# Convolution in column halves with products from SBUF, and a PSUM pool that hands out single banks or pairs

## The chip, the cores and the metric

The kernel runs on one core of one Trainium2 chip. The metric is the device time of one execution in microseconds (us). Each run executes a kernel several times, next to executions of the kernel before on the same chip. An execution is slow when it is over 1.5% above the fastest of its kernel. Ratios and intervals use the fast executions alone.

Words used below: TensorE (PE in the profile) multiplies matrices, PEld is its weight load; VectorE is DVE, ScalarE is ACT, GpSimd is POOL, SyncE is SP. PSUM is TensorE's output memory of eight banks; a bank holds 512 fp32 values per partition. An eviction is a copy of a result out of PSUM. FFN 1 is the feed-forward part's first matrix product, followed by GELU on ScalarE; FFN 2 is its second, followed by SiLU on ScalarE.

## The reference

It joins a long convolution (by FFT, over 2048 tokens and 640 columns) and a feed-forward part of 1728 hidden columns. Cut to what matters:

```python
xn = layernorm(x)                                   # x: 2048 x 640, bf16
k_shift = sum_t shift(k, t) * shift_k[t]            # 4 taps
kv  = k_shift * v
y   = irfft(rfft(kv, 4096) * rfft(ssm_k, 4096))[:2048] + kv * ssm_D
h   = gelu(xn @ w1 + b1)
g   = silu(h @ w2 + b2)
out = x + xn * y * g
```

A warning about correctness. With the given inputs, the reference's output equals x exactly in bf16: the added term is too small to change any element. So "correct" says nothing about the convolution.

## The kernel before

The FFT is done as matrix products in stages. Stage 1 transforms k and u (u is kv) from SBUF, and the results go through scratch memory in HBM (scrK, scrU) because the axes have to change places. Stage 2 transforms them further; VectorE multiplies the spectra; inverse stage 1 (i1) and, through a third scratch (scrC), inverse stage 2 (i2) follow. All operations stand in one list, and a string named ORDER fixes the engine and the order of each, and the slot of every buffer. The framework puts in the semaphores.

The parts that matter here:

```python
ps_t = [psum.tile([P, 2, 512], F32, name="ps%d" % i) for i in range(4)]   # 4 tiles of 2 banks
ps_pool = Pool(ps_t, name="ps")                      # every user takes a whole pair
...
def f1_pair(c, ft0):                                 # FFN 1: two groups, both banks of one pair
    ps = Buf(pool=ps_pool, parts=2)
    for i in range(2):
        ... matmuls of group ft0 + i into ps.v[0:M, i, :], then GELU from ps.v[0:M, i, :]
...
def f2(c, q):                                        # FFN 2: two groups into one pair, one SiLU over both
    ps = Buf(pool=ps_pool, parts=2)
    ...
    op("silu", "ACT", ... in_=ps.v[:, :, 0:H] ..., reads=[ps], writes=[sl])
...
    op("prod", "DVE", ... in0=ps.v[:, None, :, 0:w].to_broadcast([P, 2, 2, w]), in1=kin.v[...], op=ALU.mult)
    ...                                              # product with the u spectrum straight from PSUM
    def i1(...):                                     # inverse stage 1: four terms summed on TensorE
        for n_, (qi, m, tb) in enumerate(((0, 0, 0), (0, 1, 2), (1, 0, 2), (1, 1, 1))):
```

## Time and profile before

| | before |
|---|---|
| median, range in the rounds with the changed kernel | 215.74 us, 214.17 to 217.03 (4 executions) |
| span of the profiled execution, granted TensorE clock | 214.4 us, 0.967 |
| TensorE busy, idle | 179.4 us, 35.0 us |

The page gives the busy time of each engine with its share of the span, then the chain of work that ended last, then groups of instructions. A group reads: line, engine, operation, output<-input, shapes, count | busy us, mean ns of one | idle time before them and what ended it. From the page of the kernel before:

```profile
PE 179.4 (84%) x1660; PEld 90.4 (42%) x1660; DVE 166.2 (78%) x233; ACT 126.5 (59%) x163; POOL 37.6 (18%) x62
...
PE 58%; DVE 20%; DMA 11%; issue 5%; ACT 3%; POOL 0%; DVEq 0%; ACTq 0%; POOLq 0%
...
L617 DVE TENSOR_TENSOR k_all<-ps,k_all 128x1920 bf16<-128x1920 f32 (+1 forms) x22 | 45.5, 2093 | 20.1 <-PE ps L596 17.1
...
L420 ACT ACTIVATE hT<-ps,b_f 128x512 bf16<-128x512 f32 (+1 forms) x28 | 18.2, 685 | 11.0 <-PE ps L416 11.0
```

TensorE is busiest. L617 is the spectral product that the change takes apart; L420 is GELU in the paired form. The next view cuts the execution into three stretches (columns: start:end, length, busy us of each engine with the number of instructions, granted clock, DMA share, GB/s):

```profile
0.00:19.40 19.40, 7.41 (x52) 4.53 (x53) 16.04 (x43) 11.81 (x14) 8.99 (x19) 1.00 0.89 335
19.40:191.40 172.00, 160.24 (x1504) 78.72 (x1505) 130.66 (x157) 113.24 (x148) 28.57 (x44) 0.98 0.71 232
191.40:214.40 23.00, 11.76 (x107) 7.20 (x106) 19.54 (x34) 1.41 (x2) 0.00 (x0) 0.84 0.70 264
```

The first FFN matmul starts at 19.43 us. Start and tail are thin for TensorE. The middle is dense, 160.2 of 172.0 us.

### The profile page before, as it was taken

To read this page: it belongs to the slowest core of one execution; us is meant where nothing else is said; L and a number is where in the kernel's file an instruction comes from. 1 tells how busy PE (TensorE), PEld (TensorE's weight loads), DVE (VectorE), ACT (ScalarE), POOL (GpSimd) and SP (SyncE) were. 2 spreads that over 40 slices of the span, in tenths; PEclk is the share of its full clock that TensorE was granted. 3 is DMA by queue.
4 is the path that set the end of the run, shared out by engine and by line. 5 is a ranking of instruction groups with operands and counts; after the bars stand their busy time and mean duration, and the time that the engine had idled before them with its cause. 6 is when DMAs were issued, how large, how long until landed. Compare 5 with 4: busy or idle time off the path is not lost.

```text
span 214.4 us, 4137 instructions
## 1 busy us (share of the span) xinstructions
PE 179.4 (84%) x1660; PEld 90.4 (42%) x1660; DVE 166.2 (78%) x233; ACT 126.5 (59%) x163; POOL 37.6 (18%) x62
## 2 busy tenths in 40 slices
PE   0448999979988999998999899698999968999810
PEld 0314443633335665564443333233565523666500
DVE  6997998959889999964218997967756887029994
ACT  5298455877788977589554555868765764111100
POOL 7055000402252252324000020012100121100000
PEclk9999999999999999999999999999999995999985
DMA  5999998994379988949681749187980515599555
GB/s 165 373 418 412 413 356 203 361 387 172 144 214 369 242 247 206 255 151 343 214 276 27 250 144 303 27 272 257 292 278 6 199 49 192 160 415 409 207 199 198
DMA packets 28021, 52.54 MB, mean 245 GB/s; under 512 B 10081, under 2 KB 20834, under 8 KB 27874
## 3 DMA queue, kind: packets, MB, share of 16 engines
q1 hardware_dynamic: 23952, 35.89, 51.6%
q0 software_dynamic: 3904, 16.39, 20.3%
q8 instruction: 13, 0.21, 0.4%
q14 instruction: 6, 0.05, 0.1%
q10 hardware_dynamic: 146, 0.00, 0.0%
HBM read 31.95 MB, written 18.35 MB: 235 GB/s over the span
## 4 chain that ended last, share of the span: by engine, by line
PE 58%; DVE 20%; DMA 11%; issue 5%; ACT 3%; POOL 0%; DVEq 0%; ACTq 0%; POOLq 0%
PE ps L465 24%; PE ps L431 14%; PE ps L416 10%; DMA scrK<-mm 7%; DVE xn L656 5%; DVE k_all L617 5%; PE ps L629 4%; PE ps L596 3%; PE ps L497 3%; DMA x<-in_x_dram 2%; DVE stats L370 2%; DVE x L448 2%; DMA b_r<-in_b_dram 1%; DVE kT L448 1%; DVE mm L234 1%
## 5 line engine op out<-in xcount | busy, mean ns | idle before, releaser
L465 PE MATMUL ps<-w_sb,hT 128*128 128x320 bf16 x448 | 66.5, 303 | 1.4 <-ACT hT L420 0.8
L617 DVE TENSOR_TENSOR k_all<-ps,k_all 128x1920 bf16<-128x1920 f32 (+1 forms) x22 | 45.5, 2093 | 20.1 <-PE ps L596 17.1
L465 PEld LDWEIGHTS <-hT 128*128 128x128 bf16 x448 | 42.4, 99 | 24.5 <-issue 8.4
L234 ACT CAST mm<-ps 128x640 bf16<-128x640 f32 x55 | 35.1, 699 | 12.6 <-PE ps L497 6.9
L416 PE MATMUL ps<-xnT,w_sb 128*128 128x512 bf16 (+1 forms) x140 | 34.0, 393 | 1.9 <-ACT hT L420 1.6
L431 PE MATMUL ps<-xnT,w_sb 128*128 128x512 bf16 (+1 forms) x140 | 32.2, 380 | 0.6 <-ACT hT L439 0.5
L420 ACT ACTIVATE hT<-ps,b_f 128x512 bf16<-128x512 f32 (+1 forms) x28 | 18.2, 685 | 11.0 <-PE ps L416 11.0
L469 ACT ACTIVATE sl<-ps 128x640 bf16<-128x640 f32 x16 | 11.3, 707 | 21.5 <-PE ps L465 13.7
L439 ACT ACTIVATE hT<-ps,b_f 128x1024 bf16<-128x1024 f32 (+1 forms) x14 | 15.5, 1112 | 13.2 <-PE ps L431 13.1
L234 ACT CAST v_all<-ps 128x960 bf16<-128x960 f32 (+1 forms) x19 | 17.2, 947 | 9.0 <-PE ps L629 9.0
L416 PEld LDWEIGHTS <-w_sb 128*128 128x128 bf16 (+1 forms) x140 | 13.3, 101 | 20.0 <-issue 7.5
L638 POOL DMA_DIRECT2D scrC<-v_all x11 | 8.2, 749 | 73.0 <-ACT v_all L234 33.7
L431 PEld LDWEIGHTS <-w_sb 128*128 128x128 bf16 (+1 forms) x140 | 13.0, 98 | 18.0 <-issue 4.4
L234 ACT CAST k_all<-ps 128x960 bf16<-128x960 f32 (+1 forms) x16 | 14.2, 927 | 5.1 <-PE ps L596 4.1
L497 PE MATMUL ps<-kT,W 64*128 64x320 bf16 x64 | 8.9, 337 | 9.3 <-DMA kT<-in_kT_dram 8.3
L629 PE MATMUL ps<-k_all,tabs 32*64 32x480 bf16 (+1 forms) x352 | 13.3, 397 | 3.7 <-DVE k_all L617 1.9
L501 POOL DMA_DIRECT2D scrK<-mm x16 | 8.8, 550 | 42.8 <-ACT mm L234 35.3
L470 DVE TENSOR_TENSOR xn<-xn,sl 128x640 bf16<-128x640 bf16 x16 | 7.6, 484 | 9.9 <-ACT sl L469 9.9
L497 PEld LDWEIGHTS <-W 64*128 64x128 bf16 x128 | 4.8, 95 | 20.7 <-issue 11.6
L656 DVE TENSOR_TENSOR xn<-ps,xn 128x640 bf16<-128x640 f32 x16 | 12.6, 816 | 1.1 <-PE ps L652 1.1
L501 POOL DMA_DIRECT2D scrU<-mm x16 | 8.9, 556 | 19.0 <-ACT mm L234 14.7
L521 DVE TENSOR_TENSOR mm<-k_all,mm 128x2560 bf16<-128x2560 bf16 x8 | 11.9, 1490 | 0.2
(75 smaller groups left out, 176.7 us busy)
## 6 DMA issues: line engine op xcount, KB each, us to landing
scrK<-mm POOLq DMA_DIRECT2D x16, 320.0 KB, 6.6
scrU<-mm POOLq DMA_DIRECT2D x16, 320.0 KB, 3.3
k_all<-scrK SPq DMA_DIRECT2D x10, 480.0 KB, 3.9
v_all<-scrU SPq DMA_DIRECT2D x10, 480.0 KB, 4.7
scrC<-v_all POOLq DMA_DIRECT2D x10, 480.0 KB, 3.7
mm<-scrC SPq DMA_DIRECT2D x6, 640.0 KB, 6.4
kT<-in_kT_dram SPq DMA_DIRECT2D x4, 640.0 KB, 8.8
v_all<-in_v_dram SPq DMA_DIRECT2D x4, 640.0 KB, 7.1
```

The costliest lines, as they stand in the source:

```text
L234: (nc.scalar.copy if e == "ACT" else nc.vector.tensor_copy)(out=out_, in_=in_)
L416: nc.tensor.matmul(out=ps.v[0:M, i, :], lhsT=w1_sb[:, ft, t, 0:M], rhs=xnT_b[c].v[:, t, :], start=(t == 0), stop=(t == DT - 1))
L420: op("gelu", "ACT", lambda e, i=i, ft=ft, M=M: nc.scalar.activation(out=hT_b[c].v[0:M, ft, :], in_=ps.v[0:M, i, :], func=ACT.Gelu_apprx_ta ...
L431: nc.tensor.matmul(out=ps.v[0:M, i, :], lhsT=w1_sb[:, ft, t, 0:M], rhs=xnT_b[c + i].v[:, t, :], start=(t == 0), stop=(t == DT - 1))
L439: nc.scalar.activation(out=o, in_=s, func=ACT.Gelu_apprx_tanh, bias=b1_f[0:M, ft:ft + 1], scale=1.0)
L465: nc.tensor.matmul(out=ps.v[:, h, 0:H], lhsT=hT_b[c].v[0:M, ft, q * P:(q + 1) * P], rhs=w2_sb[0:M, ft, h * H:(h + 1) * H], start=(ft == 0) ...
L497: nc.tensor.matmul(out=ps.v[:, h, 0:H], lhsT=W[r, j, :], rhs=src[r, j, cs], start=True, stop=True)
L501: op("s1st" + kind, "POOL", lambda e: nc.gpsimd.dma_start(out=by_k1(scr)[:, 2 * j:2 * j + 2, :], in_=o.v), reads=[o], writes=[scr_b[j]], s ...
L521: op("kv2", "DVE", lambda e: tt(out=kt_t, in0=win(2, 2), in1=wbc(2, 2), op=ALU.mult), reads=kb + [wb_b], writes=[kvt_b])
L617: op("prod", "DVE", lambda e, ps=ps, qb=qb, kin=kin, w=w: nc.vector.tensor_tensor(out=qb.v[:, 0:4 * w].rearrange("p (i r w) -> p i r w", i ...
L629: nc.tensor.matmul(out=pc[g // 2].v[64 * r:64 * r + 64, g % 2, 0:w], lhsT=I1[tb][32 * g:32 * g + 32, :], rhs=qs[qi].v[32 * g:32 * g + 32, ...
L656: op("ym", "DVE", lambda e, j=j, ps=ps: nc.vector.tensor_tensor(out=hv(xn[:, j, :]), in0=ps.v[:, :, 0:H], in1=hv(xn[:, j, :]), op=ALU.mult ...
```

## The change

Its intent: let half of the columns go through the whole convolution while the other half is still being transformed; take the sum of the four inverse terms off TensorE by combining the products on VectorE; and use PSUM more finely, so that an FFN group of one bank no longer takes a pair. The schedule string is new throughout. The core of the diff, with cuts marked by "...":

```diff
+class Banks(Pool):
+    def __init__(self, pairs):
+        super().__init__([p[:, i, :] for p in pairs for i in range(2)])
+        self.pairs, self.flex = pairs, True
+
+    def view(self, slot, width):
+        return self.views[slot] if width == 1 else self.pairs[slot // 2]
...
     ps_t = [psum.tile([P, 2, 512], F32, name="ps%d" % i) for i in range(4)]
-    ps_pool = Pool(ps_t, name="ps")
+    banks = Banks(ps_t)
+    def pair():
+        return Buf(pool=banks, width=2)
+    def bank():
+        return Buf(pool=banks)
...
-    def f1_pair(c, ft0):
-        ps = Buf(pool=ps_pool, parts=2)
+    def ffn1(c, ft):
+        ps = bank()
...
     def f2(c, q):
-        ps = Buf(pool=ps_pool, parts=2)
         for h in range(2):
+            ps = bank()
...
+            op("silu", "ACT", ... in_=ps.v[:, 0:H], func=ACT.Silu), reads=[ps], writes=[sl[h]])
...
-            op("prod", "DVE", ... in0=ps.v[:, None, :, 0:w]..., in1=kin.v[...], op=ALU.mult), reads=[ps, kin], ...)
+                op("s2ev", "ACT|DVE", ... evict(...ps.v[:, :, 0:2 * w]), reads=[ps], writes=[src[t]])
+            def prod(e, t=t):
...
+                for r in range(2):
+                    nc.vector.tensor_tensor(out=q[:, r], in0=uu[:, r, :, None, :]..., in1=ku[:, r, None, :, :]..., op=ALU.mult)
+            def comb(e, t=t):
...
+                nc.vector.tensor_tensor(out=q[:, :, 0, 0], in0=q[:, :, 0, 0], in1=q[:, :, 1, 1], op=ALU.subtract)
+                nc.vector.tensor_tensor(out=q[:, :, 1, 0], in0=q[:, :, 1, 0], in1=q[:, :, 0, 1], op=ALU.add)
...
-    # in words: scratch rows of 640 columns; 16 stores each to scrK and scrU
+    # in words: scratch rows of 320 columns, by column half; 32 stores each
```

Also new are ten warm-up matmuls on TensorE, and the LayerNorm statistics of two row blocks on ScalarE.

## The prediction

> **What bounds it now.** TensorE is 84% busy (page, part 1), VectorE 78%, ScalarE 59%; the chain of waits is 58% TensorE, 20% VectorE, 11% DMA. By stretches of the timeline: from 0 to 19.4 us TensorE is busy for only 7.4 us (LayerNorm on VectorE, then transposes, before the first FFN matmul); from 19.4 to 191.4 us it is busy 160.2 of 172.0 us; from 191.4 us to the end only 11.8 of 23.0 us, because the chain there is VectorE: 16 multiplications of the inverse transform (816 ns each), the last sums (485 ns each) and stores. In the middle stage VectorE is uneven: 1.6 of 10 us busy from 100 to 110 us, 9.9 of 10 from 120 to 130 us, since the convolution starts only when all of scrU is stored and the inverse only when all of scrC is.
>
> **What the change does, costed.**
> 1. Products: 20 of 2154 ns plus 2 of 1486 ns, reading fp32 PSUM (45.6 us). The Trainium skill, "VectorE: DVE Perf Modes" (Why PSUM operands drop a tier), caps fp32 PSUM operands at 1x; the trace agrees: 128x1920 takes 2154 ns, while an all-bf16 SBUF multiplication of 128x2560 takes 1490 ns. From the SBUF durations (484 ns at 640, 820 at 1280, 1490 at 2560) I estimate 0.65 us for 960 and 0.40 us for 480: products 28 us, new combinations 17 us. Sum 45 us: VectorE saves nothing here.
> 2. New evictions of the u spectra: 22 of about 0.96 us on ScalarE or 1.15 us on VectorE; ScalarE gets 16 of them, and 8 more i1 evictions move to VectorE. Two statistics move to ScalarE. Net VectorE +10 us (to about 175 us), ScalarE +18 us (to about 145 us; separate GELUs and SiLUs included).
> 3. Inverse stage 1: 352 matmuls become 176, about 15 us busy to 8-9 us. The transposes for G move to DMA (-1.9 us). TensorE about 172 us, warm-up matmuls apart.
> 4. Column halves: half 0 goes through the convolution and half of the inverse while half 1 is still transformed. The schedule puts the last FFN matmuls at the very end, so the 20 us VectorE tail lies under them; only SiLU, multiplication, sum and store (about 4.5 us) stay.
> 5. Start: first-stage transforms of k fill TensorE before the FFN; two statistics on ScalarE. FFN starts perhaps 4 us earlier.
> 6. DMA: scratch rows of 1280 B become 640 B. The skill's "DMA: Bandwidth & Descriptors" (Specifications) names 512 B as the line-rate minimum, so I expect a mild loss; no trace here shows it yet. Descriptor issues on GpSimd rise from 43 to 76.
>
> **On the critical path.** TensorE idle now is 35 us: 12 start, 12 middle, 11 tail. After: about 8, 12, 5. So 172 + 25 = 197 us, about 18 us (9%) less: tail 6-8, matmuls 7, start 4. VectorE at 90% is the second limit and keeps the middle gaps from vanishing.
>
> **Prediction.** 197 us, 8 in 10 within 188 to 207. Faster by over 2%: 0.91; within 2%: 0.06; slower: 0.03.
>
> **Right or wrong by the profile.** Product near 0.65 us for 128x960 (bf16 SBUF); VectorE busy 170-180 us, ScalarE 140-150, TensorE 168-177 without warm-up; the last FFN matmul within 6 us of the end; first FFN matmul at 14-16 us; VectorE without the empty stretches around 100 and 180 us.
>
> **What would make it wrong.** Small rows making DMA the limit (it is already full from 10 to 40 us); VectorE, not TensorE, pacing the middle; lower granted clock when TensorE is denser; flexible banks letting TensorE wait less than I assume, towards 185 us.

## More of the kernel before

TensorE waits for GELU very little; the list of waits gives engine, tile and line, what it waited for, total us, times, and the longest:

```profile
PE ps L416 <- ACT hT L420: 1.6, 2, 1.2
PE ps L465 <- ACT hT L420: 0.8, 1, 0.8
```

## The result and the profile after

| | before | changed |
|---|---|---|
| median, range | 215.74 us, 214.17 to 217.03 | 225.76 us, 224.73 to 226.96 (4 executions) |
| span, clock of the profiled execution | 214.4 us, 0.967 | 224.9 us, 0.967 |
| TensorE busy, idle | 179.4, 35.0 us | 180.6, 44.3 us |

The ratio is 1.047 (95% interval 1.0379 to 1.0561). It is slower, where 9% less was predicted. A ratio here is the mean time of one kernel's fast executions over that of the other's in the same rounds, so not quite the ratio of the medians.

The page of the changed kernel, the lines that answer to those above:

```profile
PE 180.6 (80%) x1846; PEld 90.9 (40%) x1846; DVE 173.3 (77%) x301; ACT 142.0 (63%) x212; POOL 67.8 (30%) x102
...
L458 PE MATMUL ps<-xnT,w_sb 128*128 128x512 bf16 (+1 forms) x280 | 69.3, 388 | 16.0 <-ACT hT L462 15.5
...
L462 ACT ACTIVATE hT<-ps,b_f 128x512 bf16<-128x512 f32 (+1 forms) x56 | 37.1, 692 | 13.1 <-PE ps L458 12.9
...
L650 DVE TENSOR_TENSOR k_all<-v_all,xtra 128x960 bf16<-128x960 bf16 x16 | 9.8, 652 | 0.8 <-ACT v_all L260 0.6
```

The product at L650 costs 652 ns, as estimated, and VectorE and ScalarE are busy for as long as predicted. So it isn't the work that was mis-sized; it's the waiting. The FFN 1 matmuls (L458) now stand idle 16.0 us, nearly all of it for GELU. The list of TensorE's waits begins:

```profile
PE ps L458 <- ACT hT L462: 15.5, 16, 3.1
PE ps L523 <- ACT W L382: 6.7, 1, 6.7
PE ps L490 <- ACT sl L494: 5.1, 3, 3.5
```

Three stretches again, cut at the first (20.59 us) and the end of the last FFN matmul:

```profile
0.00:20.60 20.60, 9.34 (x51) 4.22 (x52) 17.46 (x50) 15.29 (x23) 10.37 (x28) 1.00 0.89 328
20.60:220.20 199.60, 171.28 (x1796) 86.65 (x1795) 154.85 (x250) 126.32 (x188) 57.41 (x76) 0.97 0.79 228
220.20:224.90 4.70, 0.00 (x0) 0.00 (x0) 0.98 (x2) 0.44 (x1) 0.00 (x0) 0.87 0.51 174
```

The tail did shrink to 4.7 us. The loss is in the middle: 28.3 us idle (199.6 - 171.3) against 11.8 before. ScalarE is no bottleneck there, being busy 126 of 200 us. So why does TensorE wait for it? The timeline around the worst place shows it (columns: start, busy us, engine, line, operation, then in brackets the idle time before and its releaser). Lines of other engines are left out:

```profile
127.47 2.32 PE L458 MATMUL ps<-xnT,w_sb 128*128 128x512 bf16 x10
...
129.82 0.69 ACT L462 ACTIVATE hT<-ps,b_f 128x512 bf16<-128x512 f32 x1 [0.70 <-PE ps L458]
...
130.56 1.24 PE L458 MATMUL ps<-xnT,w_sb 128*128 128x512 bf16 x5
...
131.84 0.69 ACT L462 ACTIVATE hT<-ps,b_f 128x512 bf16<-128x512 f32 x1 [1.33 <-PE ps L458]
...
134.12 0.71 ACT L462 ACTIVATE hT<-ps,b_f 128x512 bf16<-128x512 f32 x1
...
134.88 2.26 PE L458 MATMUL ps<-xnT,w_sb 128*128 128x512 bf16 x5 [3.08 <-ACT hT L462]
```

I matched each instruction to its operation and bank. Two FFN 1 groups run up to 129.78 us: one in bank 7, done at 128.71, then one in bank 6. The GELU at 129.82 reads bank 7. ScalarE was free from 129.12, yet it starts only when the group of bank 6 has ended. The group at 130.56 goes into bank 7. The GELU at 131.84 reads bank 6, which was complete at 129.78; it starts just as the group of bank 7 ends, at 131.80. The group at 134.88 goes into bank 6. The GELU of bank 6 had ended at 132.53; the group starts just after the GELU of bank 7 ended, at 134.83. So 2.3 us of that 3.08 us wait (132.53 to 134.83) are for the neighbouring bank. Banks 6 and 7 are the two halves of one tile, ps3.

The pause costs again through the clock: the five matmuls after it take 2.26 us, where five alike took 1.24 us at 130.56; the granted clock from 134.88 to 137.10 us is 0.52. The Trainium skill, "TensorE: Matmul & The Clock Gate" (Part 1), describes a clock that falls to half after an idle window of about 3.4 us; the trace agrees in the factor (2.26 / 1.24 = 1.8), but here a pause of 3.08 us was enough. That fits TensorE's busy time: without its ten warm-ups (4.5 us) it is 176.1 us, where the same matmuls take 169.9 us in e9 of experiment 7, at a mean clock of 0.997. In the window from 130 to 140 us it is busy for 5.14 of 10 us, at a granted clock of 0.83, while no other engine is near full:

```profile
130.00:140.00 10.00, 5.14 (x71) 1.78 (x52) 4.92 (x11) 5.89 (x8) 0.16 (x1) 0.83 0.59 147
```

I then counted, in the instructions as built, the waits of an FFN operation for the GELU, SiLU or matmuls of *another* group; they are called foreign waits below. In the changed kernel there are 53: 13 of a GELU and 9 of a SiLU for a later group's matmuls, and 21 of an FFN 1 group and 10 of an FFN 2 group for another group's GELU or SiLU. The kernel before has 8. (A recount from fresh builds, by a rule that may differ in detail, gives 52, with 8 of a SiLU, and 10.)

### The profile page after: what moved, and what is told of

Read it like the earlier page. It is cut to its first block, busy times and chain, and to the rows that moved or that the text cites. A ratio compares the mean times of both kernels' runs of the same rounds, so it can differ in the third digit from the quotient of the medians.

```text
span 224.9 us, 4726 instructions
## 1 busy us (share of the span) xinstructions
PE 180.6 (80%) x1846; PEld 90.9 (40%) x1846; DVE 173.3 (77%) x301; ACT 142.0 (63%) x212; POOL 67.8 (30%) x102
## 2 busy tenths in 40 slices
DMA packets 41095, 53.09 MB, mean 236 GB/s; under 512 B 12721, under 2 KB 32722, under 8 KB 41074
## 5 line engine op out<-in xcount | busy, mean ns | idle before, releaser
L458 PE MATMUL ps<-xnT,w_sb 128*128 128x512 bf16 (+1 forms) x280 | 69.3, 388 | 16.0 <-ACT hT L462 15.5
L458 PEld LDWEIGHTS <-w_sb 128*128 128x128 bf16 (+1 forms) x280 | 26.3, 99 | 52.0 <-issue 27.1
L462 ACT ACTIVATE hT<-ps,b_f 128x512 bf16<-128x512 f32 (+1 forms) x56 | 37.1, 692 | 13.1 <-PE ps L458 12.9
L494 ACT ACTIVATE sl<-ps 128x320 bf16<-128x320 f32 x32 | 13.5, 439 | 32.8 <-PE ps L490 32.8
L531 POOL DMA_DIRECT2D scrU<-mm x32 | 22.4, 738 | 35.9 <-ACT mm L260 32.4
L260 ACT CAST v_all<-ps 128x960 bf16<-128x960 f32 (+2 forms) x29 | 26.2, 918 | 9.4 <-issue 4.3
L260 DVE CAST v_all<-ps 128x960 bf16<-128x960 f32 (+2 forms) x17 | 18.0, 1058 | 17.8 <-PE ps L668 11.5
L531 POOL DMA_DIRECT2D scrK<-mm x32 | 23.3, 837 | 14.0 <-ACT mm L260 13.9
L260 DVE CAST mm<-ps 128x640 bf16<-128x640 f32 x10 | 8.1, 821 | 8.7 <-PE ps L523 6.6
L552 DVE TENSOR_TENSOR mm<-k_all,mm 128x2560 bf16<-128x2560 bf16 x8 | 11.9, 1490 | 0.2
L549 DVE TENSOR_TENSOR mm<-k_all,mm 128x2560 bf16<-128x2560 bf16 x8 | 11.9, 1485 | 0.1
L650 DVE TENSOR_TENSOR kT<-v_all,k_all 128x960 bf16<-128x960 bf16 (+1 forms) x14 | 8.2, 630 | 3.9 <-ACT v_all L260 3.6
L650 DVE TENSOR_TENSOR k_all<-v_all,xtra 128x960 bf16<-128x960 bf16 x16 | 9.8, 652 | 0.8 <-ACT v_all L260 0.6
```

Of the source, the lines that this page charges most:

```text
L260: (nc.scalar.copy if e == "ACT" else nc.vector.tensor_copy)(out=out_, in_=in_)
L458: nc.tensor.matmul(out=ps.v[0:M, :], lhsT=w1_sb[:, ft, t, 0:M], rhs=xnT_b[c].v[:, t, :], start=(t == 0), stop=(t == DT - 1))
L462: op("gelu", "ACT", lambda e: nc.scalar.activation(out=hT_b[c].v[0:M, ft, :], in_=ps.v[0:M, :], func=ACT.Gelu_apprx_tanh, bias=b1_f[0:M, f ...
L494: op("silu", "ACT", lambda e, h=h, ps=ps: nc.scalar.activation(out=sl.v[:, h * H:(h + 1) * H], in_=ps.v[:, 0:H], func=ACT.Silu), reads=[ps ...
L531: nc.gpsimd.dma_start(out=by_h(scr)[:, b, :, j, :], in_=o.v[:, b])
L549: op("kv2", "DVE", lambda e: tt(out=kt_t, in0=win(0, 2), in1=wbc(0, 2), op=ALU.mult), reads=kb + [wb_b], writes=[kvt_b], extra=[u for b in ...
```

## The experiments

**Theory A.** The framework guards a PSUM tile as a whole: it makes the users of any part of the tile wait for one another, in the order of the list. As long as every user takes a whole pair, that is right. When single banks are handed out, two unrelated users of one tile wait for each other.
**Rival B.** The 640-byte scratch rows and the 33 more DMA issues on GpSimd cost the time.
**Rival C.** The start: the first FFN matmul came at 20.59 us, not at 14 to 16, after TensorE waited 6.7 us for W.

### 1. All eight banks in one tile (e1_after_banks)

In the instructions of small test builds I had seen that a tile of two to seven banks is guarded as a whole, while one tile of all eight is guarded bank by bank. (The builds of the kernels here bear it out for two and four banks and for eight.) So the guard can be made fine without touching the schedule:

```diff
-    ps_t = [psum.tile([P, 2, 512], F32, name="ps%d" % i) for i in range(4)]
+    ps_all = psum.tile([P, 8, 512], F32, name="ps_all")
+    ps_t = [ps_all[:, 2 * i:2 * i + 2, :] for i in range(4)]
```

> The changed kernel with one edit: PSUM is declared as one tile of 8 banks instead of four tiles of 2, so that the semaphores guard single banks; same schedule, same instructions. Theory A (an FFN group waits for the other bank of its pair: in the changed kernel 18 GELU or SiLU instructions start 0.5 to 3.3 us late and TensorE waits 15.5 us for GELU and 5.1 us for SiLU): TensorE's waits for GELU and SiLU fall from 20.6 us to under 8 us and the time falls by 8 to 20 us, to 206 to 218 us. Rival B (DMA with 640 B rows paces the middle): the waits move to another place and the time stays at 222 to 227 us.

Measured: 203.96 us median (202.05 to 207.53, four executions, two of them slow), ratio to before 0.9344 (0.9291 to 0.9398). That is 21.8 us below the changed kernel, a little more than the 8 to 20 us expected. None of the foreign waits is left in the built instructions. From its page, its list of waits and its three stretches:

```profile
PE 174.2 (87%) x1832; PEld 88.5 (44%) x1846; DVE 171.4 (86%) x301; ACT 141.0 (71%) x212; POOL 68.4 (34%) x102
```

```profile
PE ps_all L524 <- ACT W L383: 6.3, 1, 6.3
...
PE ps_all L459 <- ACT hT L463: 0.3, 1, 0.3
```

```profile
0.00:21.60 21.60, 9.95 (x51) 4.22 (x51) 17.56 (x50) 15.25 (x23) 10.72 (x28) 0.69 0.91 335
21.60:195.30 173.70, 164.24 (x1784) 84.30 (x1796) 152.83 (x250) 125.34 (x188) 57.71 (x75) 0.98 0.87 259
195.30:199.90 4.60, 0.00 (x0) 0.00 (x0) 0.98 (x2) 0.44 (x1) 0.00 (x0) 0.93 0.52 179
```

The wait for GELU falls from 15.5 to 0.3 us. The middle falls from 199.6 to 173.7 us for the same operations in the same order: 18.9 us less idle and 7.0 us less busy. (This trace lacks the records of 14 FFN 1 matmuls. At about 0.24 us each, an estimate from the busy time of its group over its count, up to 3.4 us of what it counts as idle is really busy.) That the rest of the busy time is the clock's is argued, not shown. The window that was worst in the changed kernel, 130 to 140 us, now has TensorE busy for 9.79 of 10 us at full clock:

```profile
130.00:140.00 10.00, 9.79 (x181) 4.79 (x181) 9.29 (x20) 9.46 (x15) 2.40 (x3) 1.00 0.94 263
```

This version beats both kernels. It also shows that the schedule was sound; it had been built for banks that are independent. Rival C falls as the cause of the loss: in this version the first FFN matmul comes even later (21.60 us), with 6.3 us of waiting for W, and yet the time is 21.8 us less.

### 2. The same edit in the kernel before (e2_before_banks)

> Control: the same edit in the kernel before, where every group that shares a pair is read as a pair or follows the pair's order; only 8 waits for the other bank were found. Theory A: 213 to 216 us, within 1% of the kernel before. If it falls by more than 2%, the pair guard was no cost of the change.

Measured: 215.38 us, ratio 0.9937 (0.9875 to 0.9999). Where the users take whole pairs, the finer guard is worth half a per cent.

### 3. Small rows in the kernel before (e3_before_rows)

The edit keeps the kernel before and stores its scratch by column half, with one DMA per half:

```diff
-    scrK = dram.tile([P * N2, D], BF16, name="scrK")
+    scrK = dram.tile([2, P * N2, H], BF16, name="scrK")        # scrU and scrC alike
...
-    nc.gpsimd.dma_start(out=by_k1(scr)[:, 2 * j:2 * j + 2, :], in_=o.v)
+    [nc.gpsimd.dma_start(out=by_h(scr)[:, b, :, j, :], in_=halves(o.v)[:, :, b, :]) for b in range(2)]
```

Only the size and the number of the transfers matter here.

> The kernel before with the DMA side of the change alone: scratch rows of 640 B in two column halves, and one DMA for each half (48 more issues on GpSimd and SyncE); its numbers are wrong on purpose, because the row order in scratch does not fit the tables. Theory A: within 2% (212 to 219 us). Rival B: slower by 4% or more, 224 us and above, with the DMA share of busy time above 80%.

Measured: 215.46 us, ratio 0.9963 (0.9911 to 1.0014). Its page shows the change took effect:

```profile
PE 178.3 (84%) x1649; PEld 90.6 (42%) x1660; DVE 166.5 (78%) x233; ACT 126.4 (59%) x163; POOL 72.9 (34%) x105
...
DMA packets 45925, 52.55 MB, mean 246 GB/s; under 512 B 11249, under 2 KB 39762, under 8 KB 45778
```

The packets rose from 28021 to 45925, more than the 41095 of the changed kernel, and GpSimd's time nearly doubled, and the kernel lost no time. Rival B falls for this schedule; for the changed one experiment 1 settles it, where the same transfers run in 21.8 us less. The Trainium skill, "DMA: Bandwidth & Descriptors" (Specifications), names 512 B as the least transfer for line rate, and 640-byte rows lie above it. No run here measures the line rate, but the smaller and more numerous transfers were not free for the DMA engines: for the same 52.5 MB, their queues' packets took 80.2% of 213.4 us where they had taken 71.9% of 214.4 us, about 11% more (so Rival B's mark, a share above 80%, did come, without the loss of time).

### 4. A coarser guard (e4_quads)

If A holds, making the guard coarser must hurt more. The changed kernel with its schedule as it is, but two tiles of four banks:

```diff
-    ps_t = [psum.tile([P, 2, 512], F32, name="ps%d" % i) for i in range(4)]
+    ps_h = [psum.tile([P, 4, 512], F32, name="psh%d" % i) for i in range(2)]
+    ps_t = [ps_h[i // 2][:, 2 * (i % 2):2 * (i % 2) + 2, :] for i in range(4)]
```

> The changed kernel with the same schedule, but its eight PSUM banks declared as two tiles of four banks instead of four tiles of two. Theory A (a wait is kept for a whole PSUM tile, so a group of one bank waits for its neighbours in the tile): a coarser tile means more neighbours, so slower still, at least 230 us against 225.8 us, with more waits of TensorE for hT and sl than the 24 us of the changed kernel. Rival (the 22 us that the one-tile version saved came from something else in how the banks are addressed or placed, not from the size of the guard): two tiles should lie near or below the changed kernel, 204 to 226 us.

Measured: 331.36 us (330.75 to 335.79), ratio 1.5321 (1.5198 to 1.5444). The other engines were busy for as long as in the changed kernel; the time went into waits of every kind, and into the clock, which fell to 0.838:

```profile
PE 215.9 (65%) x1846; PEld 101.4 (31%) x1846; DVE 175.1 (53%) x301; ACT 144.7 (44%) x212; POOL 67.8 (21%) x102
```

```profile
PE psh L459 <- ACT hT L463: 13.9, 13, 3.1
PE psh L459 <- ACT mm L261: 7.1, 4, 3.4
PE psh L459 <- DVE v_all L261: 6.5, 4, 3.7
PE psh L491 <- ACT sl L495: 6.5, 4, 3.1
```

An FFN 1 group now waits for evictions of the convolution (mm, v_all) too, which it has nothing to do with except a tile in common. In all, TensorE's waits for hT and sl add up to 36.9 us in its list, against 21.0 us in the changed kernel's. "At least 230" was far too low, but the direction and the kind of waits are those of A. The rival in that expectation falls.

### 5. The coarser guard in the kernel before (e8_before_quads)

The edit of experiment 4, in the kernel before.

> The kernel before with its eight PSUM banks declared as two tiles of four banks instead of four of two. Theory A (the guard covers a whole tile): slower than 215.5 us, by 20 us or more, since two pairs with different work now share a guard; with the one-tile control (0.994 of before) this shows that the kernel before lost nothing at pairs because its operations take whole pairs, and not because it is immune. Rival (only the changed kernel suffers, for another reason in its new operations): within 2% of 215.5 us.

Measured: 361.6 us, ratio 1.6816 (1.6663 to 1.6969). That is 146 us more, where "20 us or more" was expected. So the kernel before isn't immune; it merely had users that fit its tiles. TensorE's two longest waits are for products and for evictions of stage 1; some are again between unlike stages, as FFN 2 (L466) waiting for an eviction of stage 1 (mm):

```profile
PE psh L597 <- DVE k_all L618: 17.5, 6, 6.2
PE psh L498 <- ACT mm L235: 16.7, 23, 2.3
...
PE psh L466 <- ACT mm L235: 7.1, 7, 2.7
```

Together, as ratios to the kernel before:

| guard | schedule of before | schedule of the change |
|---|---|---|
| each bank | 0.994 | 0.934 |
| pair | 1 | 1.047 |
| four banks | 1.682 | 1.532 |

The first row compares the two schedules without foreign waits: the change is worth 6%. The second row is what was measured at first, with its sign turned.

### 6. The start (e5_stats, e6_order, e7_both)

These three start from the version of experiment 1 and test C. In e5 the statistics of two row blocks go back to VectorE:

```diff
-    nc.scalar.activation(out=xn[:, j, :], in_=xs(j), func=ACT.Identity, accum_out=acs[:, j, 0:1])
-    nc.scalar.activation(out=xn[:, j, :], in_=xs(j), func=ACT.Square, accum_out=acs[:, j, 1:2])
...
+    for h in range(2):
+        nc.vector.bn_stats(out=stats[:, j, h, :], in_=xs(j)[:, h * H:(h + 1) * H])
+    nc.vector.bn_aggr(out=mv[:, j, :], in_=stats[:, j, :, :])
```

> The changed kernel with all eight banks in one PSUM tile, and the statistics of rows 1 and 3 put back from ScalarE onto VectorE. If the two statistics on ScalarE and the table load between them and the sine delay W and with it the first-stage transform (6.3 us of TensorE waiting for W), then W comes about 3 us earlier, the first k transform starts near 8.5 us instead of 11, and the wait for W falls to about 3 us. The time then falls by 0 to 2 us from 204 us, since VectorE gets about 2 us more at the start, which could hold up the first FFN matmul just as long.

In e6 only the first entries of the schedule string change places (row loads x1, x3, x0, x2 first, the statistics of x2 right after, small tables and later statistics behind them).

> The changed kernel with all eight banks in one PSUM tile, and only the order of the first operations changed: rows that the first FFN group needs are loaded and normalised first, the small tables and later statistics come after. If VectorE's order at the start decides when the FFN starts, the first FFN matmul comes near 17 us instead of 20.6 us, and the time falls by 1 to 3 us from 204 us. If the start is set by the loads of weights or by TensorE's own transforms, nothing moves (within 1 us).

In e7 both edits are made.

> The changed kernel with all eight banks in one PSUM tile, with both edits of the start (statistics of rows 1 and 3 on VectorE, and the new order). If the two causes add, first FFN matmul near 15.5 us and 199 to 201 us. If they compete for VectorE, no better than the better of the two.

| | median time, ratio | first k transform | first FFN matmul | TensorE's longest wait before the first FFN matmul, in total |
|---|---|---|---|---|
| e1 | 203.96, 0.9344 | 10.74 us | 21.60 us | W 6.3 us |
| e5 | 203.82, 0.9403 (0.9317 to 0.9488) | 9.13 us | 22.10 us | kT load 7.4 us |
| e6 | 203.27, 0.9345 (0.924 to 0.9451) | 10.56 us | 20.33 us | W 6.1 us |
| e7 | 202.73, 0.9361 (0.9269 to 0.9453) | 8.94 us | 20.92 us | kT load 6.8 us |

None is faster than e1 beyond the intervals (the means of the fast executions are 202.4 us for e1 and 203.2, 202.6 and 202.3 us for e5, e6 and e7), and the first FFN matmul stays between 20 and 22.1 us. So the hoped-for branch of each expectation missed; what held is the other branch of e6 (nothing moves) and of e7 (no better). (The profile of e5 fell in a slow execution; its start is read with that in mind.) W does come earlier without the statistics on ScalarE, but then TensorE waits for the load of kT about as long as it had waited for W. From e7's list:

```profile
PE ps_all L522 <- DMA kT<-in_kT_dram: 6.8, 2, 4.5
...
PE ps_all L439 <- DVE xn L423: 2.2, 1, 2.2
```

Taking one wait away uncovers the next, so the statistics on ScalarE alone don't hold the start. VectorE's order is not cleared, though. The wait of 2.2 us for xn, which ends at 19.35 us, is TensorE's last before the first FFN matmul; it is for the normalisation of the fourth row block. Its last input, rstd, was there at 11.43 us, and in the built instructions it carries no wait of its own. Yet it runs at 18.72 us, because in VectorE's order the statistics of later rows (which wait 1.3 us for their load) and a multiplication of the convolution (which waits 0.6 us for its own) stand before it. From e7's timeline:

```profile
10.71 0.72 POOL L420 TENSOR_TENSOR rstd<-veps,mhalf 128x2 f32<-128x2 f32 x1
...
17.31 1.49 DVE L548 TENSOR_TENSOR mm<-k_all,mm 128x2560 bf16<-128x2560 bf16 x1 [0.64 <-DMA mm<-in_wsh_dram]
18.72 0.57 DVE L423 TENSOR_SCALAR xn<-x,mv,rstd 128x640 bf16<-128x640 bf16 x1
```

The new order of e6 and e7 left that operation where it was. From 10 us on the DMA engines are full (share 1.01 to 1.03 in the windows 10 to 20 and 20 to 30 us of these runs), so the loads may hold the start too. No run moved this operation, or had fewer or earlier loads, so what each is worth stays open.

### 7. The warm-up matmuls (e9_nowarm, e10_banks_again, e11_nowarm_again, e12_order_nowarm)

In three of four executions of e1 the mean clock was 0.942 to 0.947, and in the profiled one it was 0.50 from 10 to 20 us, although the ten warm-ups are there to keep it up. So e9 leaves them out:

```diff
-    op("warm", "PE", lambda e, ps=ps: nc.tensor.matmul(out=ps.v[:], lhsT=xtra[:, 0:P], ...), reads=[z_b], writes=[ps])
+    op("warm", "PE", lambda e, ps=ps: None, reads=[z_b], writes=[ps])
```

> The changed kernel with all eight banks in one PSUM tile, and its ten warm-up matmuls left out. TensorE busy falls by about 4.5 us. If they hold the granted clock up at the start, the first transforms and FFN matmuls run slower and the time rises by 0.5 to 2 us from 204 us; if the 6 us wait for W undoes them anyway (the granted clock was 0.5 from 10 to 20 us in spite of them in the one-tile run), the time stays within 1% of 204 us.

Measured: 200.37 us (199.93 to 202.67), ratio 0.9318 (0.9247 to 0.939), with the clock at 0.994 to 1.0 in all four. That looked like a gain of 1.8% over e1's median. But e1 had run in another batch, two of its executions were slow (between the means of the fast ones it is 0.8%), and the two intervals overlap. So three versions were run side by side, six executions each:

> The one-tile version of the changed kernel once more, in the same rounds as the next two, as their reference: 202 to 205 us, with the mean granted clock 0.94 to 0.95 in most executions, as in its first run (three of four executions).

> The same without warm-up matmuls, repeated beside it. If the warm-ups followed by a pause of 6 us set off the low granted clock at 10 to 30 us (theory from the first look: 0.994 to 1.0 in four of four executions without them, 0.942 to 0.947 in three of four with them), then 200 to 201.5 us, 1 to 2% below its neighbour with them, and clock above 0.99 in most executions. If the difference between the two batches was the chip or chance, the two lie within 0.5% and show the same clocks.

> The same without warm-up matmuls and with both edits of the start (statistics of rows 1 and 3 on VectorE, new order). The start edits alone gained nothing that could be told from noise (0.934 and 0.936 of before against 0.934); if that was because the low clock at 10 to 30 us ate the gain, this lies 1 to 3 us below the version without warm-ups, at 197.5 to 199.5 us; if the loads of k set the start, it lies within 1 us of it.

| | median (range) | ratio (interval) | mean of the fast executions | clocks |
|---|---|---|---|---|
| e10, with warm-ups | 203.02 (201.61 to 204.82) | 0.939 (0.9343 to 0.9438) | 202.6, five | 0.945 to 1.0 |
| e11, without | 202.79 (200.44 to 205.17) | 0.9359 (0.93 to 0.9418) | 201.9, four | 0.98 to 1.0 |
| e12, without, e7's start | 202.36 (201.12 to 206.6) | 0.937 (0.9322 to 0.9417) | 202.2, five | 0.979 to 1.0 |

The three can't be told apart: their means lie within 0.4%, less than an interval. So e9's gain is not confirmed. e10's own expectation missed as well: one execution in six had the low clock, not most. Among these versions a low mean clock was recorded only with warm-ups (never below 0.979 in the 16 executions without), but it hardly costs: in e10 the execution at 0.945 took 203.08 us, and that at 0.992 took 203.41. The traces show why the record misleads here. In e9, six transforms of the first stage took 0.98 us at 11.30, 15.39 and 19.99 us at a recorded clock of 1.00, just as in e1 (at 10.74, 16.09 and 20.68 us) at 0.50 from 10 to 20 us; six alike took 0.58 us in e10 at 20.00 us. So TensorE was slow at the start without warm-ups too, and only the record differs. e12 was slow there as well (its first ten FFN 1 matmuls took 4.51 us, e7's 4.58), so whether the slow start hid a gain of the start edits is not settled. For the time of the kernel, no difference was measured between leaving the warm-ups in and taking them out.

## Why the prediction was wrong

The step that failed is an unwritten one under "TensorE idle ... After: about 8, 12, 5": that a group waits only for what it reads or overwrites. Under the guard per pair it also waits for its neighbour in the tile, and the 12 us of the middle became 28.3. The prediction named the flexible banks as a risk, but with the wrong sign, "letting TensorE wait less than I assume, towards 185 us". The tile declaration was in the kernel and unchanged, and a change from users of pairs to users of single banks under it was the thing to look at.

| step of the prediction | with the guard per pair | with the guard per bank (e1) |
|---|---|---|
| products 0.65 us, combinations 0.40 us | 652 and 402 ns | 651 ns (product) |
| VectorE 175, ScalarE 145 us | 173.3, 142.0 | 171.4, 141.0 |
| TensorE 172 us without warm-ups | about 176 | 169.9 (e9, no warm-ups) |
| TensorE idle at the start 8 us (warm-ups as idle) | 15.0 | 15.4 |
| TensorE idle in the middle 12 us | 28.3 | 9.5 at most |
| tail 5 us | 4.7 | 4.6 |
| 197 us, 188 to 207 | 225.76, outside | 203.96, inside |

The idle times are the stretch less TensorE's busy time in it. The ten warm-ups are busy for 4.5 us; 3.75 us of that lie in the first stretch (seven at 3.17 us, one of 0.58) and are counted as idle there.

- **Products and VectorE: right.** "VectorE saves nothing here" holds. The Trainium skill, "VectorE: DVE Perf Modes" (Why PSUM operands drop a tier), gave the reason why the products get cheaper per element from SBUF, and the trace agrees: 128x1920 from PSUM is 2154 ns, 128x960 from SBUF is 652 ns, so 1.12 against 0.68 ns per column. The combinations eat the difference.
- **Matmuls: right in sum, wrong in parts.** Inverse stage 1 fell from 13.3 to about 8 us (5.8 + 2.2). But the stage-2 transforms became 704 matmuls of half the width, and rose from 15.2 us (8.4 + 6.8) to 17.5 us (8.7 + 5.6 + 3.2). The prediction left that out.
- **Start: wrong.** "FFN starts perhaps 4 us earlier" did not happen in any version (20.3 to 22.3 us against 19.43). What holds it is open; experiment 6 clears the statistics on ScalarE by themselves, but not VectorE's order or the loads. In the version with the fine guard this is the largest miss, 7.4 us of idle time (15.4 - 8).
- **Tail: right,** 4.7 us.
- **DMA: no loss of time where "a mild loss" was expected** (experiment 3), although the DMA engines were occupied about 11% longer.
- **Middle: wrong by 16 us of idle time,** plus the busy time that the lower clock adds. One line, the tile declaration, gives it back: the middle stretch is 25.9 us shorter in e1. That cause is shown by experiment 1, and by the doses of experiments 2, 4 and 5.

## What to carry to other kernels

When buffers get finer than the objects on which the synchronisation is kept, change the objects as well: make the unit of allocation the unit of the guard. In a trace, look for an engine that waits for another one that is half idle, and match the times to the bank: an operation that starts exactly when its neighbour's work ends, long after its own input was ready, waits for the wrong thing. And compare small gains only within one batch: 1.8% between the medians of two batches was gone when both versions ran side by side. A mean granted clock is no safe sign by itself either: compare how long like matmuls took.

## What the Trainium skill lacked or had wrong

- "PSUM — Partial Sum Buffer" (PSUM bank collisions raise a hardware error) has the rule to guard PSUM by bank and quadrant, "by bank is the simple version". The runs agree, but the page has no word on a guard that is too coarse, and none on its price: guards of one, two and four banks gave 0.934, 1.047 and 1.532 of the time before for one schedule, and 0.994, 1 and 1.682 for another.
- "Perfetto Trace Analysis" (Optimizing Tensor Performance, Matmuls) advises to rotate independent groups through different banks so that evictions overlap. The changed kernel does rotate, and still TensorE waited 15.5 us for GELU, against 0.3 us with a guard per bank. The page lacks the condition that the banks be guarded apart, and a hint how such a wait looks in a trace.
- "TensorE: Matmul & The Clock Gate" (Part 1) gives about 3.4 us as the idle window after which the clock halves. In the changed kernel shorter waits were enough: the granted clock was 0.52 after a wait of 3.08 us (five matmuls took 2.26 against 1.24 us) and 0.50 after one of 2.17 us (2.29 us for five, at 63.51 us), while it stayed at 1.00 after waits of 1.74 and 1.60 us (at 139.83 and 190.65 us).
